# Sketch matrices loaded from GpSimd's queue, keys first on the two other load queues, eleven clock fillers in one group, and a new order of steps

## The chip, the core and the metric

The kernel runs on one core of one Trainium2 chip. The core has five engines that run side by side, each through its own list of instructions in order: TensorE (PE, matmuls; PEld is its loading of weights), VectorE (DVE), ScalarE (ACT), GpSimd (POOL) and SyncE (SP). Data comes from and goes to the chip's memory by DMA. A DMA is issued by an instruction on an engine (here on SP, ACT, and after the change also on POOL), and the issuing instruction takes time on that engine. The metric is the device time of one execution in microseconds (us).

## What is computed

Attention by polynomial sketches, followed by a feed-forward layer with a rational activation.

```python
# q, k, v: (4, 4, 1088, 32); S1, S2: (8, 32); w_in: (128, 2048); w_out: (2048, 128); float32
def phi(x):                                   # 64 features of a token
    a = np.einsum('rd,bhsd->bhsr', S1, x)
    b = np.einsum('rd,bhsd->bhsr', S2, x)
    return np.einsum('bhsi,bhsj->bhsij', a, b).reshape(*x.shape[:-1], 64)
q_p, k_p = phi(q), phi(k)
kv = np.einsum('bhsf,bhsd->bhfd', k_p, v)
z = np.sum(k_p, axis=2)
num = np.einsum('bhsf,bhfd->bhsd', q_p, kv)
den = np.einsum('bhsf,bhf->bhs', q_p, z)[..., None] + 1e-06
x = (num / den), heads side by side           # (4352, 128)
h = x @ w_in
P = a[0] + a[1]*h + a[2]*h**2 + a[3]*h**3
Q = 1.0 + abs(b[0])*abs(h) + abs(b[1])*h**2
out = (P / (Q + 1e-06)) @ w_out               # (4352, 128)
```

## The kernel before

The work comes in two interleaved streams. The attention stream goes batch by batch: keys are transposed on DVE (`kt`, L254), sketched with S1 and S2 on PE (`ks`, L261), one half is copied by ACT (`kc`, L268), the two halves are multiplied to features on DVE (`kf`, L273), and PE multiplies features with values (`kp`, L302); ACT copies the result into `kvz` (`kk`, L312). Queries go a similar way in blocks: transpose (`qt`, L325), sketch (`qs`, L338), copy (`qc`, L345 and L348), features (`qf`, L354 and L357), products with `kvz` (`qp`, L365), the division (`qd`, `qi`, `qx`), a transpose back on PE (`qb`, L391) and a copy into `xT` (`qk`, L398).

The feed-forward stream goes over 17 units of tokens and hidden columns: `h` is the matmul with w_in (L455, four parts a unit), `e` its copy to bf16 on ACT (L461), `u`, `w`, `y` build the denominator on DVE, `ln` and `ex` invert it on ACT, `pa` (ACT) or `pd` (DVE) build part of the numerator, `s`, `m`, `v`, `x` multiply on DVE, `G` is the matmul with w_out (L588), and `st` transposes and stores.

Nothing is scheduled by a planner when the kernel is built. The order of all steps is written out in the string `ORDER`, a list of `name:number` entries that a loop at the end runs through; since each engine works in order, `ORDER` fixes the order on every engine. Loads are entries as well, and are issued from SP: `lk`, `lq`, `lv` for keys, queries and values, `lx:0` and `lx:1` for the halves of w_in, `lw:0` and `lw:1` for the halves of w_out. `wo:0` to `wo:5` turn a half of w_out into one of three bf16 copies, on ACT or DVE as `W_ENG` says (1 is ACT): even numbers read the half of `lw:0`, odd numbers that of `lw:1`. `ba` makes |b| on ACT.

Ahead of the list stands a fixed opening. It loads S1 (ACT's queue) and S2 (SP's queue), then the first batch's keys in three loads, queries and values. The matrices are transposed on DVE (`sT`, L195) and masked into `S12` (L200), which the key sketches need; POOL writes the masks and some ones and zeros, and then makes `S21` (L206) and `SAB` (L212) for the query sketches. These DVE steps come ahead of every entry of `ORDER`.

`tn:i` is a group of `TURNS[i]` filler matmuls on a tile of zeros (L170) whose result nobody reads. Before the change `tn:0`, `tn:1`, `tn:4` and `tn:5` stand in the opening with 12, 2, 1 and 2 of them, 17 in all, ahead of the first key sketch on PE.

Of the kernel before, what the change touches and what calls it, by code (L numbers as in the profile page):

```python
# [16 lines left out]
PSUM = bass.MemoryType.PSUM  # L17


TURNS = (12, 2, 0, 0, 1, 2, 0, 0, 0)  # L20
ORDER = """
tn:0 lw:1 lq:0 kt0:0 lw:0 kt1:0 lx:1 tn:1 kt2:0 lx:0 tn:4 kt3:0 tn:5 lk:1 ks0:0 qt:0 qt:1 ks1:0 kc0:0 ks2:0 kf0:0
kc1:0 kf1:0 qs:0 kc2:0 kf2:0 kp0:0 qc:0 kp1:0 ba:0 qf:0 kp2:0 wo:3 qs:1 kk:0 lv:1 qt:3 qp:0 qt:2 qc:1 wo:1 lq:1 qf:1
qs:2 qd:0 qi:0 qc:2 qp:1 qx:0 qf:2 wo:0 qb:0 qp:2 qd:1 wo:4 qk:0 qi:1 h3:0 qx:1 qd:2 wo:5 wo:2 h2:0 e3:0 kt1:1 kt0:1
h0:0 e2:0 qi:2 lk:2 pa1:0 u1:0 qs:3 w1:0 h1:0 qx:2 y1:0 qc:3 e0:0 qb:2 qb:1 qt:4 e1:0 ks1:1 qt:5 qk:2 u0:0 qk:1 qs:4
ln1:0 h2:1 w0:0 qt:6 y0:0 kc1:1 ex1:0 h0:1 kf1:1 e2:1 ks0:1 s1:0 e0:1 h1:1 m1:0 kc0:1 pa0:0 kf0:1 h3:1 lq:2 kt0:2 e1:1
x1:0 e3:1 h0:2 ln0:0 u1:1 h2:2 qf:3 w1:1 qc:4 e0:2 qp:3 e2:2 kt1:2 y1:1 ex0:0 h1:2 s0:0 h3:2 ln1:1 m0:0 kp1:1 e3:2
x0:0 qd:3 e1:2 qi:3 pd0:1 ex1:1 G0:0 qx:3 lv:2 u1:2 G1:0 ln0:1 G2:0 w1:2 lk:3 G3:0 y1:2 qs:5 kk:1 ex0:1 qb:3 G4:0
ks0:2 qk:3 qf:4 G5:0 kc0:2 ln0:2 kf0:2 qp:4 s0:1 qc:5 G0:1 qd:4 ex0:2 qi:4 qx:4 G1:1 s1:1 qb:4 ks1:2 qk:4 s0:2 pa1:1
h2:3 kt1:3 m0:1 kc1:2 h3:3 qt:7 e2:3 m1:1 kf1:2 h0:3 e3:3 ln1:2 x1:1 qs:7 h1:3 x0:1 e0:3 st:0 m0:2 h2:4 e1:3 pd1:2  # L30
pa0:2 h3:4 u1:3 qf:5 e2:4 kp1:2 w1:3 qc:7 ex1:2 x0:2 h0:4 e3:4 s1:2 pa0:3 qt:9 qp:5 y1:3 e0:4 h1:4 qd:5 m1:2 ln0:3
G2:1 qi:5 x1:2 G3:1 e1:4 kt0:3 lv:3 G4:1 ex0:3 u1:4 ks0:3 G5:1 m0:3 pa1:3 G0:2 w1:4 G1:2 ln1:3 qx:5 G2:2 y1:4 qb:5
G3:2 qk:5 ex1:3 h0:5 m1:3 kk:2 v0:3 ln0:4 h2:5 s1:3 G4:2 e0:5 ex0:4 qf:7 h1:5 x0:3 e2:5 qs:6 s0:4 qc:6 e1:5 h3:5 pd0:4
pa1:4 m0:4 h1:6 v1:3 x0:4 e3:5 G5:2 e1:6 u1:5 qp:7 ln1:4 qt:8 st:2 h3:6 w1:5 ex1:4 x1:3 G0:3 e3:6 h0:6 y1:5 pa0:5 lq:3
G2:3 s1:4 h2:6 e0:6 m0:5 qd:7 ln0:5 G3:3 qi:7 m1:4 G5:3 e2:6 qf:6 qs:8 ex0:5 x1:4 G0:4 G1:4 u1:6 qc:8 ln1:5 qp:6 v0:5
qx:7 w1:6 qb:7 qd:6 pa0:6 G2:4 qi:6 G3:4 qx:6 y1:6 qb:6 qk:7 G4:4 qk:6 ex1:5 h3:7 m0:6 pa1:5 G5:4 s1:5 h1:7 e3:7 qt:10
h2:7 st:4 e1:7 m1:5 ln0:6 h0:7 x0:5 e2:7 x1:5 e0:7 h3:8 qf:8 ex0:6 u1:7 qs:9 v0:6 h1:8 qc:9 ln1:6 w1:7 ks1:3 s0:6 e1:8
G0:5 y1:7 kc1:3 ex1:6 qp:8 h2:8 pd1:6 kc0:3 e3:8 s1:6 ln0:7 h0:8 kf0:3 e2:8 m1:6 G2:5 ex0:7 x0:6 G3:5 G4:5 kf1:3 qd:8
e0:8 qs:10 G5:5 ln1:7 qi:8 u1:8 kp1:3 qx:8 pa0:7 w1:8 qf:9 qb:8 G0:6 qk:8 y1:8 qc:10 ex1:7 h3:9 s0:7 h2:9 e3:9 s1:7
ln0:8 h0:9 m0:7 e2:9 x1:6 G2:6 e0:9 h1:10 x0:7 ex0:8 pd1:7 h1:9 m1:7 pa0:8 s0:8 G3:6 e1:9 u1:9 G0:7 qt:11 ln1:8 qp:9  # L40
qt:12 u0:9 m0:8 h3:10 e1:10 w1:9 qd:9 ex1:8 qf:10 h2:10 x0:8 e3:10 x1:7 G4:6 kk:3 e2:10 h0:10 y1:9 pa0:9 w0:9 qp:10
qi:9 y0:9 e0:10 G1:7 qx:9 qd:10 ln0:9 qi:10 s1:8 qb:9 G5:6 u1:10 G2:7 qk:9 ex0:9 G3:7 qx:10 m1:8 qb:10 G4:7 qk:10
pd1:8 ln1:9 qs:11 s0:9 h1:11 qc:11 w1:10 ex1:9 h0:11 m0:9 e1:11 x1:8 G5:7 e0:11 h3:11 y1:10 pa1:9 G0:8 s1:9 e3:11
h2:11 ln0:10 x0:9 h0:12 m1:9 e2:11 pd0:10 ex0:10 h1:12 u1:11 x1:9 G1:8 ln1:10 G2:8 w1:11 G3:8 e0:12 s0:10 G0:9 e1:12
y1:11 G4:8 ex1:10 G5:8 G1:9 m0:10 ln0:11 G2:9 qf:11 h2:12 s1:10 ex0:11 x0:10 h3:12 pa1:10 m1:10 qs:12 s0:11 G3:9 qc:12
e2:12 G4:9 pd0:11 ln1:11 G5:9 m0:11 qp:11 x1:10 e3:12 G0:10 x0:11 qd:11 ex1:11 G1:10 qi:11 u1:12 G2:10 pa1:11 qx:11
G3:10 w1:12 qb:11 G4:10 qk:11 s1:11 pa0:12 h1:13 y1:12 h3:13 e1:13 m1:11 ln0:12 h2:13 st:6 x1:11 ex0:12 G5:10 qf:12
G0:11 st:10 e3:13 qp:12 s0:12 e2:13 st:8 h0:13 ln1:12 m0:12 u1:13 h2:14 e0:13 x0:12 ex1:12 u0:13 h3:14 w1:13 e2:14
w0:13 y1:13 e3:14 h1:14 qd:12 pa1:12 y0:13 h0:14 s1:12 e1:14 qi:12 m1:12 G1:11 e0:14 G2:11 qx:12 ln1:13 u1:14 G3:11
x1:12 qb:12 G4:11 ex1:13 w1:14 G5:11 G0:12 qk:12 pd0:13 ln0:13 h0:15 y1:14 ex0:13 h2:15 pd1:13 s1:13 e0:15 G1:12 s0:13  # L50
ln0:14 G2:12 h3:15 m1:13 e2:15 m0:13 ex0:14 h1:15 x1:13 x0:13 e3:15 G3:12 e1:15 G4:12 s0:14 ln1:14 G0:13 u1:15 G5:12
m0:14 h2:16 pa0:14 w1:15 h3:16 ex1:14 st:12 y1:15 G1:13 e2:16 e3:16 h1:16 x0:14 ln0:15 u2:16 u3:16 h0:16 w2:16 s1:14
ex0:15 w3:16 G2:13 y2:16 pd0:15 e1:16 G0:15 y3:16 e0:16 G3:13 s0:15 pa1:14 u0:16 G1:15 m0:15 G4:13 ln1:15 w0:16 G5:13
m1:14 G0:14 ex1:15 y0:16 G1:14 G2:14 v1:14 ln0:16 G3:14 pd1:15 s1:15 ex0:16 x0:15 x1:14 G2:15 ln2:16 m1:15 G5:14
ex2:16 s0:16 G0:16 pa0:16 x1:15 G3:15 st:14 ln3:16 m0:16 G4:15 ex3:16 s2:16 G1:16 x0:16 pa2:16 G5:15 m2:16 pa3:16
G2:16 s3:16 G3:16 x2:16 G4:16 st:15 G5:16 m3:16 G6:16 G7:16 x3:16 G8:16 st:16
""".split()
W_ENG = (1, 1, 0, 0, 0, 1)
P_ON_ACT = (1, 1, 0, 1, 1, 0, 1, 1, 0, 1, 1, 1, 1, 0, 1, 0, 1, 0, 1, 1, 0, 1, 0, 1, 1, 1, 0, 0, 1, 1, 0, 0, 1, 1)
SPLIT_A = (0, 9, 13, 16)  # L60
QUARTER = (16,)
LX = 4
TAIL = 2
WIDE_S = (3, 5)
WIDE_M = (5,)
# [4 lines left out]
def kernel(  # L70
# [13 lines left out]
    nc = tc.nc  # L84
# [53 lines left out]
    s_raw = []  # L138
    for i, s_in in enumerate((S1, S2)):
        t = consts.tile([128, D], FP, name=f"s_raw{i}")  # L140
        (nc.scalar, nc.sync)[i].dma_start(out=t, in_=bass.AP(tensor=s_in.tensor, offset=s_in.offset,
                                                             ap=[[0, 16], [D, R], [1, D]]))
        s_raw.append(t)
    nc.scalar.dma_start(out=k0.rearrange("p (m x) -> p m x", m=NM)[:, :, 0:4 * D],
                      in_=bass.AP(tensor=k.tensor, offset=k.offset, ap=[[S * D // 32, 128], [W, NM], [1, 4 * D]]))
    nc.sync.dma_start(out=k0[:, 0:km].rearrange("p (m x) -> p m x", m=NM - 1)[:, :, 4 * D:],
                        in_=k0_src[:, 0:km].rearrange("p (m x) -> p m x", m=NM - 1)[:, :, 4 * D:])
# [19 lines left out]
    def turn(i, cols=512):  # L167
        idle_ps = bank()
        for _ in range(TURNS[i]):
            nc.tensor.matmul(idle_ps[:, :cols], lhsT=idle[:, 0:128], rhs=idle[:, :cols], start=True, stop=True)  # L170
# [22 lines left out]
    for i in range(2):  # L193
        t = consts.tile([128, D], FP, name=f"sT{i}")
# [14 lines left out]
    for i in range(2):  # L209
        t = consts.tile([128, 2, R, R], FP, name=f"SAB{i}")  # L210
# [15 lines left out]
    def bank():  # L226
        return att.tile([128, 512], FP, name="att_ps")
# [211 lines left out]
    t1 = n_tok % TC  # L439
    last = TC // TAIL  # L440
    for t0, tl in [(0, t1)] * (t1 > 0) + [(t, TC) for t in range(t1, n_tok - TC, TC)] + [(t, last) for t in range(n_tok - TC, n_tok, last)]:
# [226 lines left out]
    for step in ORDER:  # L668
        name, i = step.split(":")
        i = int(i)  # L670
# [47 lines left out]
```

## Time and profile before

| | |
|---|---|
| time, median of 3 runs | 272.9 us (272.5 to 273.84) |
| the profiled execution's own time | 272.58 us |
| its span | 270.8 us |
| PE, DVE, ACT, POOL busy | 258.0, 256.8, 249.1, 2.9 us |
| granted TensorE clock | 1.0 |

The span is the time from the first to the last instruction in the profile; the execution's own time lies 1.8 us above it. Busy time is the time in which an engine works on an instruction, without its waits. The timeline lists instructions in order of time, with neighbours of one kind merged into one row ("x4"), and with the idle time ahead of a row and what ended it in brackets. The chain is followed back from the last instruction, at each step to what released it.

### The profile page before, as it was taken

How to read it: one execution, taken by the hardware profiler on the slowest of the kernel's cores; microseconds unless marked ns; L12 is line 12 of the kernel's file. 1: busy time of each engine (PE TensorE's matmuls, PEld its weight loads, DVE VectorE, ACT ScalarE, POOL GpSimd, SP SyncE). 2: the span in 40 equal slices, each digit the busy share in tenths (PEclk: the TensorE clock that was granted, in tenths of full speed). 3: DMA queues.
4: the chain of work that ended last, by engine and by line, in shares of the span. 5: the costliest groups of instructions: out<-in, count | busy, mean ns of one | idle time of the engine just before them, and what ended most of it. 6: DMA issues, size and time to landing. Idle time of an engine off the chain costs nothing.

```text
span 270.8 us, 3744 instructions
## 1 busy us (share of the span) xinstructions
PE 258.0 (95%) x1401; PEld 146.6 (54%) x1401; DVE 256.8 (95%) x278; ACT 249.1 (92%) x224; POOL 2.9 (1%) x24
## 2 busy tenths in 40 slices
PE   8999999999999899999999999999999999999673
PEld 3887546854744354535464554434545357665362
DVE  3859999999999999999999999999999999999993
ACT  1379999989999999999999999999999999999990
POOL 4000000000000000000000000000000000000000
PEclk9999999999999999999999999999999999999999
DMA  6994424532180062331303000300216100020022
GB/s 164 286 321 138 118 76 125 160 84 67 47 151 21 12 143 75 81 77 26 97 8 121 5 1 6 120 7 0 64 47 93 23 0 2 0 39 0 1 41 40
DMA packets 30530, 19.55 MB, mean 72 GB/s; under 512 B 20400, under 2 KB 26672, under 8 KB 30512
## 3 DMA queue, kind: packets, MB, share of 16 engines
q1 hardware_dynamic: 28864, 18.92, 27.5%
q10 hardware_dynamic: 1648, 0.40, 0.7%
q8 instruction: 11, 0.18, 0.3%
q14 instruction: 7, 0.06, 0.1%
HBM read 16.16 MB, written 3.15 MB: 71 GB/s over the span
## 4 chain that ended last, share of the span: by engine, by line
ACT 38%; DVE 27%; PE 25%; issue 8%; DVEq 0%; ACTq 0%
ACT hh L461 11%; ACT ln L546 10%; PE h_ps L455 9%; ACT r L550 9%; ACT p L541 7%; PE att_ps L588 7%; DVE g L558 5%; DVE g L569 5%; DVE s L554 4%; DVE w L495 4%; DVE w L490 3%; PE att_ps L365 2%; PE att_ps L170 2%; PE att_ps L302 2%; DVE u L484 2%
## 5 line engine op out<-in xcount | busy, mean ns | idle before, releaser
L455 PE MATMUL h_ps<-xT,w_in_sb 128*128 128x512 f32 (+1 forms) x320 | 125.7, 536 | 2.3 <-ACT hh L461 1.9
L455 PEld LDWEIGHTS h_ps<-xT,w_in_sb 128*128 128x128 f32 x320 | 58.4, 190 | 53.2 <-issue 36.4
L461 ACT CAST hh<-h_ps 128x1024 bf16<-128x1024 f32 x68 | 67.9, 1023 | 3.1 <-PE h_ps L455 2.8
L588 PEld LDWEIGHTS <-w_out 128*128 128x128 bf16 x460 | 44.7, 98 | 46.7 <-issue 15.7
L546 ACT ACTIVATE ln<-w 128x2048 f32<-128x2048 bf16 (+1 forms) x35 | 65.8, 1880 | 0.5
L550 ACT ACTIVATE r<-ln 128x2048 bf16<-128x2048 f32 (+1 forms) x35 | 65.8, 1880 | 0.3
L541 ACT ACTIVATE p<-hh,a_sb 128x2048 bf16<-128x2048 bf16 (+1 forms) x23 | 46.7, 2036 | 0.0
L554 DVE TENSOR_TENSOR s<-hh,r 128x2048 bf16<-128x2048 bf16 (+2 forms) x33 | 40.9, 1247 | 0.3 <-ACT r L550 0.3
L495 DVE TENSOR_TENSOR w<-w,u 128x4096 bf16<-128x4096 bf16 (+2 forms) x22 | 39.3, 1792 | 0.0
L588 PE MATMUL att_ps<-g,w_out 128*128 128x512 bf16 (+1 forms) x160 | 35.0, 347 | 4.0 <-DVE g L569 3.9
L558 DVE TENSOR_TENSOR g<-hh,s 128x2048 bf16<-128x2048 bf16 (+1 forms) x30 | 35.0, 1171 | 0.1
L569 DVE TENSOR_TENSOR g<-g,p 128x2048 bf16<-128x2048 bf16 (+1 forms) x30 | 34.9, 1179 | 0.1
L588 PE MATMUL att_ps<-r,w_out 128*128 128x512 bf16 (+1 forms) x160 | 34.5, 347 | 0.1
L588 PE MATMUL att_ps<-s,w_out 128*128 128x512 bf16 (+1 forms) x140 | 29.7, 342 | 0.4 <-DVE s L554 0.4
L490 DVE TENSOR_SCALAR w<-u,b_abs 128x4096 bf16<-128x4096 bf16 (+2 forms) x22 | 24.0, 1096 | 0.1
L484 DVE TENSOR_SCALAR u<-hh 128x4096 uint16<-128x4096 uint16 (+2 forms) x22 | 21.3, 973 | 0.4 <-ACT hh L461 0.2
L365 PEld LDWEIGHTS att_ps<-kvz,q_pT 128*128 128x128 f32 x144 | 17.7, 192 | 3.8 <-issue 1.6
L365 PE MATMUL att_ps<-kvz,q_pT 128*128 128x66 f32 x144 | 17.8, 273 | 0.4 <-ACT sk_sb L415 0.4
L302 PEld LDWEIGHTS att_ps<-v_sb,k_p 128*64 128x64 f32 (+1 forms) x288 | 8.8, 138 | 2.3 <-issue 1.5
L536 DVE TENSOR_SCALAR p<-hh,a_sb 128x2048 bf16<-128x2048 bf16 x12 | 9.7, 805 | 0.0
L273 DVE TENSOR_TENSOR k_p<-att_ps,b_sk 128x1280 f32<-128x1280 f32 (+2 forms) x8 | 9.4, 1178 | 0.0
L302 PE MATMUL att_ps<-v_sb,k_p 128*64 128x64 f32 (+1 forms) x288 | 9.3, 223 | 0.0
(60 smaller groups left out, 134.1 us busy)
## 6 DMA issues: line engine op xcount, KB each, us to landing
a_all<-sk_d SPq DMA_DIRECT2D x6, 384.0 KB
b_all<-sk_d SPq DMA_DIRECT2D x12, 192.0 KB
v_sb<-in_v_dram SPq DMA_DIRECT2D x12, 144.0 KB
k_sb<-in_k_dram SPq DMA_DIRECT2D x3, 544.0 KB
q_sb<-in_q_dram SPq DMA_DIRECT2D x3, 544.0 KB
a_all<-sk_d SPq DMA_DIRECT2D x4, 320.0 KB
b_all<-sk_d SPq DMA_DIRECT2D x8, 160.0 KB
w_out_sb_f<-in_moe_w_out_dram SPq DMA_DIRECT2D x2, 512.0 KB
```

What stands on the lines that cost most here:

```text
L365: nc.tensor.matmul(self.nd[:, o:o + 2 * KW], lhsT=self.q_p[:, c, x:x + 128], rhs=kvz[self.b % 2][:, c, :], start=True, stop=True)
L455: nc.tensor.matmul(t[:, x * tl:(x + 1) * tl], lhsT=w_in_sb[:, f * 128:(f + 1) * 128], rhs=xT[:, x_at(t0):x_at(t0) + tl], start=True, stop= ...
L461: nc.scalar.copy(out=live[i]["hh"][:, part * PW:(part + 1) * PW], in_=live[i]["h", part])
L490: nc.vector.tensor_scalar(out=t[:, c], in0=live[i]["u"][:, c], scalar1=ab1, scalar2=ab0, op0=AX.mult, op1=AX.add)
L495: nc.vector.tensor_mul(out=t[:, c], in0=t[:, c], in1=live[i]["u"][:, c])
L541: nc.scalar.activation(out=part_of(i, "p", h), in_=hh, func=ACT.Identity, scale=a3, bias=a2)
L546: nc.scalar.activation(out=t, in_=live[i]["w"][:, span(h)], func=ACT.Ln, bias=1.0 + 1e-6)
L550: nc.scalar.activation(out=part_of(i, "r", h), in_=live[i]["ln"], func=ACT.Exp, scale=-1.0)
L554: nc.vector.tensor_mul(out=part_of(i, "s", h), in0=hh, in1=part_of(i, "r", h))
L558: nc.vector.tensor_mul(out=part_of(i, "g", h), in0=hh, in1=part_of(i, "p" if horner(i, first(h)) else "s", h))
L569: nc.vector.tensor_mul(out=g, in0=g, in1=part_of(i, "s" if horner(i, first(h)) else "p", h))
L588: nc.tensor.matmul(outs[t0][:, :tl], lhsT=w_sb[y][:, f0 + x, :], rhs=part_of(i, key, h)[:, c:c + tl], start=done[0] == 0, stop=done[0] == ...
```

## The change

- S1 and S2 are both loaded from POOL's queue, ahead of everything else that the kernel puts there. The first two key loads thereby stand first on ACT's and SP's queues.
- `TURNS` has 11 fillers in `tn:0` and none elsewhere; the entries `tn:1` and `tn:5` are gone, and `tn:4` is empty.
- `ORDER` is written anew. Each step keeps its engine. A constant `SWS = 1` is added that nothing shown reads.

```diff
-TURNS = (12, 2, 0, 0, 1, 2, 0, 0, 0)
+TURNS = (11, 0, 0, 0, 0, 0, 0, 0, 0)
 ORDER = """
-tn:0 lw:1 lq:0 kt0:0 lw:0 kt1:0 lx:1 tn:1 kt2:0 lx:0 tn:4 kt3:0 tn:5 lk:1 ks0:0 qt:0 qt:1 ks1:0 kc0:0 ks2:0 kf0:0
-kc1:0 kf1:0 qs:0 kc2:0 kf2:0 kp0:0 qc:0 kp1:0 ba:0 qf:0 kp2:0 wo:3 qs:1 kk:0 lv:1 qt:3 qp:0 qt:2 qc:1 wo:1 lq:1 qf:1
-qs:2 qd:0 qi:0 qc:2 qp:1 qx:0 qf:2 wo:0 qb:0 qp:2 qd:1 wo:4 qk:0 qi:1 h3:0 qx:1 qd:2 wo:5 wo:2 h2:0 e3:0 kt1:1 kt0:1
-h0:0 e2:0 qi:2 lk:2 pa1:0 u1:0 qs:3 w1:0 h1:0 qx:2 y1:0 qc:3 e0:0 qb:2 qb:1 qt:4 e1:0 ks1:1 qt:5 qk:2 u0:0 qk:1 qs:4
+tn:0 lw:1 lq:0 kt1:0 lx:1 kt0:0 lw:0 kt2:0 lx:0 tn:4 kt3:0 lk:1 ks1:0 qt:1 ks0:0 qt:0 ks2:0 kc0:0 kc1:0 kf0:0 kf1:0
+qs:0 kc2:0 kf2:0 kp0:0 qc:0 kp1:0 qf:0 kp2:0 wo:5 qs:1 lv:1 kk:0 qt:3 qp:0 qt:2 qc:1 wo:1 lq:1 qf:1 qs:2 qd:0 qi:0
+qc:2 qp:1 qx:0 qf:2 ba:0 qb:0 qp:2 qk:0 wo:4 wo:0 wo:3 h3:0 qd:1 qd:2 wo:2 qi:1 qx:1 h2:0 qi:2 e3:0 qx:2 kt1:1 qs:3
+kt0:1 e2:0 qb:2 h0:0 qk:2 lk:2 u1:0 pa1:0 w1:0 h1:0 y1:0 qc:3 e0:0 qt:6 qb:1 qt:4 ks0:1 e1:0 qs:4 qk:1 u0:0 kc0:1
 ...
+SWS = 1
 ...
-        (nc.scalar, nc.sync)[i].dma_start(out=t, in_=bass.AP(tensor=s_in.tensor, offset=s_in.offset,
+        nc.gpsimd.dma_start(out=t, in_=bass.AP(tensor=s_in.tensor, offset=s_in.offset,
                                                              ap=[[0, 16], [D, R], [1, D]]))
```

The rest of `ORDER` holds the same entries as before, many of them a few places earlier or later.

## The prediction, made before the changed kernel was run

> **What bounds the kernel now.** I read the page first, then the busy time by stretch, the timeline of the first 26 us, and the chain of work that ended last.
>
> The page: three engines are nearly full, and GpSimd (POOL) is almost unused.
>
> ```profile
> span 270.8 us, 3744 instructions
> PE 258.0 (95%) x1401; PEld 146.6 (54%) x1401; DVE 256.8 (95%) x278; ACT 249.1 (92%) x224; POOL 2.9 (1%) x24
> ```
>
> Busy time by stretch (length, then busy us and instructions of PE, PEld, DVE, ACT, POOL, then granted clock, DMA share, GB/s): after 36 us DVE and ACT have no idle time worth naming. What can be won lies ahead of 36 us, or in the last nine.
>
> ```profile
> 0.00:17.15 17.15, 15.96 (x158) 11.44 (x158) 11.23 (x28) 6.80 (x16) 2.92 (x24) 1.00 0.88 261
> 17.15:36.00 18.85, 18.58 (x81) 12.33 (x81) 16.27 (x21) 17.18 (x19) 0.00 (x0) 1.00 0.57 151
> 120.00:150.00 30.00, 30.00 (x174) 15.26 (x173) 30.00 (x29) 29.85 (x27) 0.00 (x0) 1.00 0.23 63
> 262.00:270.80 8.80, 3.87 (x32) 3.02 (x31) 4.24 (x8) 1.59 (x2) 0.00 (x0) 1.00 0.26 38
> ```
>
> The timeline (start, duration, engine, line, what; in brackets the idle time before it and what ended it): each load's issue, the fillers (L170), the sketch matrices on DVE (L195, L200), the key transposes (L254), the query transposes (L325) and the key features (L273).
>
> ```profile
> 0.73 0.69 SPq L141 DMA_DIRECT2D s_raw<-in_S_dram  x1
> 0.74 0.64 ACTq L141 DMA_DIRECT2D s_raw<-in_S_dram  x1
> 1.19 5.45 PE L170 MATMUL att_ps<-idle 128*128 128x512 bf16 x17 [1.19 <-DVE idle L165]
> 1.41 0.60 ACTq L144 DMA_DIRECT2D k_sb<-in_k_dram  x1
> 2.90 0.49 DVE L195 STREAM_TRANSPOSE sT<-s_raw 128x32 f32<-128x32 f32 x2 [1.77 <-DMA s_raw<-in_S_dram]
> 3.31 0.30 DVE L200 TENSOR_TENSOR S<-sT,mask 128x32 f32<-128x32 f32 x2
> 4.53 1.61 PEld L170 LDWEIGHTS <-idle 128*128 128x128 bf16 x8 [0.23 <-issue]
> 4.76 1.66 DVE L254 STREAM_TRANSPOSE kT<-k_sb 128x256 f32<-128x256 f32 x4 [1.14 <-DMA k_sb<-in_k_dram]
> 6.66 0.77 DVE L325 STREAM_TRANSPOSE qT<-q_sb 128x256 f32<-128x256 f32 x2 [0.24 <-DMA q_sb<-in_q_dram]
> 7.36 1.25 DVE L273 TENSOR_TENSOR k_p<-att_ps,b_sk 128x512 f32<-128x512 f32 x2
> 8.95 1.49 DVE L273 TENSOR_TENSOR k_p<-h_ps,b_sk 128x1280 f32<-128x1280 f32 x1 [0.34 <-ACT b_sk L268]
> ```
>
> The chain (start, length, what): from the fillers on it stays on PE without a gap until 20.9 us, and then goes to ACT.
>
> ```profile
> 1.19 5.45 PE att_ps L170 x17
> 6.63 0.84 PE att_ps L261 x8
> ...
> 17.24 3.65 PE h_ps L455 x16
> 20.91 1.02 ACT hh L461
> ```
>
> So the kernel is an opening in which PE waits for nothing but its own fillers, and then some 225 us of full engines. The first key sketch starts at 6.47, while its transposed keys were there from about 5.2. A start that is earlier by x shifts all three engines by x, if nothing later is late.
>
> **Part 1: the keys go first on SP and ACT.** Two issues leave (0.69 and 0.64 us), so the first key loads are issued at 0.73 instead of 1.41 (ACT) and 1.48 (SP): 0.67 to 0.75 earlier. All that follows on these queues was spaced by issue and by the transfer stream ahead of it (the DMA share is 0.88 in the opening), so it moves too: keys landed at 4.76 and now at about 4.1, queries at 6.66 and now at 6.0, and the first w_out half, which let L625 start at 11.25, at 10.6. Later SP issues that wait for a key load to land (1.5 us in the waits of SP, before two parts of v) move with it. I take 0.65 for all.
>
> **Part 2: both sketch matrices on POOL.** No DMA of POOL is in the trace, so its cost is bounded. The two DMAs now stand one behind the other, at the head of POOL. Low end: each holds its queue as on SP and ACT (0.66), and lands as the second one did, read at 3.18, so 2.45 after its issue began: 0.73 + 0.66 + 2.45 = 3.85. High end: after two such issues a landing as slow as the queries' (issued 2.34, read 6.66, 4.3 us): 0.73 + 1.3 + 4.3 = 6.4. I take 4.4: the same bytes from the same tensor are the nearest row, but now their packets run beside the keys' instead of ahead of them. [...] No run so far shows such a DMA.
>
> On POOL, everything else stands behind these two issues, some 1.3 us: the masks (0.73 to 1.5, then to about 2.9, still ahead of the matrices that they multiply), the ones and zeros of v_sb, kvz and kT, the identity (needed at 15.9). SAB took until 1.1 us after S12 was done; it would be ready near 5.9, and the first query sketch comes at about 7.4. All hidden at these prices.
>
> **Part 3: the transposes.** DVE takes L195 and L200 in program order ahead of the keys. In the trace, from the start of the second L195 to the end of L200 was 0.43 us. So the key transposes start at T = max(4.1, 4.4 + 0.42) = 4.8, 0.04 later than before: the keys' 0.65 is lost on DVE, the sketch matrices being now what is late.
>
> **Part 4: fillers 17 to 11.** By the PEld rows the first eight start 0.427 apart, and from 4.53 on 0.216 apart. Eleven end at 4.53 + 3 x 0.216 = 5.2. The new first sketch step, ks1, needs the first transpose (T + 0.45 = 5.25). PE's own part of the gain is 6.47 - 5.25 = 1.2 us.
>
> **Part 5: what is late next.** DVE: four key transposes 1.66, two query transposes 0.77 (queries there at 6.0), key features 1.25 and 1.49: the last features end at T + 5.17, where the trace has 10.44 for T = 4.76; the saving is the waits of 0.24 (queries) and 0.34 (b_sk), since sketches now run ahead. After them come 40 of the 72 products, 2.32 x 40/72 = 1.29. The products end at T + 6.5 = 11.3; they ended at 11.95. PE alone would get there sooner (ks2 from T + 1.66, 1.12; query sketches 1.13; 32 products 1.03; sum T + 4.94), so DVE decides. Gain **0.65 us**.
>
> **Part 6: moved steps.** On ACT wo:5 (1.04) now stands ahead of kk:0, and its half of w_out lands at 10.6: kk would start at 11.65, end at 12.2, and release qp:0; PE gets to qp:0 at 11.3 + 1.13 = 12.4. Hidden, by 0.2. It leaves 17.35, where ACT had idle time, so it brings nothing. wo:3 (0.75, DVE) leaves 11.25 for the stretch after qf:2, where DVE stood idle for 2.2 us before the second batch's key transposes; those wait for their load (landed 20.39) with qi:2 and qx:2 (0.6) now ahead of them: idle time filled. qk:0 goes ahead of wo:0 (1.16) on ACT: x reaches PE earlier, but h3:0 starts when qp:2 is done, so nothing. ba:0 goes behind qc:2; b_abs is read at 22.7. On SP lx:1 goes ahead of lw:0: the w_in half is earlier, the w_out half some 1.6 us later (first read at 15.7; the load that reuses its semaphore found it landed at 13.8). After 30 us the order differs by swaps of neighbours on PE, ACT and DVE. With engines full they can remove almost nothing, and can cost where one waits; I put zero, with 0.7 us on both sides.
>
> **Sum.** h3:0, ACT's hh and all behind them come 0.65 earlier. The profiled execution took 272.58 (270.8 of span and 1.8 around it), 0.3 below the median 272.9. 272.58 - 0.65 = 271.9, at the level of the median 272.25: 272.3.
>
> **Rivals.**
>
> (a) The sketch matrices land late; slower. Place: DVE's first wait. Each us after 4.4 adds a us to T, and the gain is 5.45 - T, so the turn is a landing at 5.0; a landing at the high end, 6.4, gives T = 6.8 and costs 1.35: 274.2. At 7 it costs 1.95: 274.9. For it: two issues in a row on a queue whose price no row shows, packets beside the full key stream, small loads behind it. Against it: 16 KB landed in 2.2 us on the other queues.
>
> (b) The new order costs in the full stretch: one wait the size of L254's 2.2 us for the second batch's keys, but at a place where no engine has slack, from which all three run late: 272.3 + 2.2 = 274.5. For it: 147 of 272 DVE steps stand at another place in their order. Against: most moves are by one to five places.
>
> (c) The fillers carry more than this execution shows; faster. The rate doubled 3.3 us after the first filler. Had it done so a us later, 17 fillers would have ended 0.5 later and 11 at most 0.7 later, which T mostly hides; never, at 8.4 against 5.9. Gain 0.65 + 0.5 to 2.0: 271.7 to 270.2. [...]
>
> (d) The change does nothing: the matrices land at 5.0, the fillers' gain is eaten on DVE: 272.9.
>
> **Numbers.** 0.5%, about what a measurement of this kernel can tell from no change, is 1.4 us. Forecast 0.44 and (d) 0.10; (a) 0.20, (b) 0.13, (c) 0.13. Faster by over 0.5%: three quarters of (c), and a quarter of the forecast, where the low landing (T = 4.3, gain 1.15) meets the order's 0.7: 0.21. Slower: three quarters of (a), and most of (b): 0.26. Within: 0.53. Range 271.0 to 274.6: it leaves out the far ends of (a), (b) and (c).
>
> **What would show it.** Right: first L144 issue near 0.74; L195 of the second matrix at about 4.4 and L254 at 4.8; 11 fillers ending near 5.2; last key features ending near 10.0; products at 11.3; first L455 near 16.5; hh at 20.3; full engines after. Wrong: an L195 after 5.0, a PE gap after the fillers with slow sketches, kvz (L312) held by wo:5, or new waits on DVE or ACT after 36 us.

## The result, and the profile after

| | before | after |
|---|---|---|
| time, median (range) | 273.27 us (272.5 to 273.84, 4 runs) | 277.97 us (277.31 to 278.85, 4 runs) |
| the profiled execution | 272.58 us, span 270.8 | 278.45 us, span 276.7 |
| ratio, after over before | | 1.0168, 95% interval 1.0146 to 1.019 |

The kernel became 1.7% slower. The forecast was 272.3 us, and its range ended at 274.6.

The page of the kernel after: span and engines, the granted clock in 40 slices, and POOL's queue. The engines do as much as before (PE 259.2 us, DVE 256.2, ACT 249.2). What differs is the clock: 0.5 and 0.7 in the second and third slice, that is from 7 to 21 us, and full afterwards. The queue `q0` is the new one of POOL: 64 packets and 0.03 MB.

```profile
span 276.7 us, 3730 instructions
PE 259.2 (94%) x1380; PEld 149.5 (54%) x1395; DVE 256.2 (93%) x278; ACT 249.2 (90%) x224; POOL 4.1 (1%) x26
PEclk9579999999999999999999999999999999999999
q0 software_dynamic: 64, 0.03, 0.0%
```

The timeline of the opening after (start, duration, engine, line, what; idle time before it and what ended it). All lines are one higher than before.

```profile
0.74 0.50 ACTq L145 DMA_DIRECT2D k_sb<-in_k_dram  x1
1.19 3.88 PE L171 MATMUL att_ps<-idle 128*128 128x512 bf16 x11 [1.19 <-DVE idle L166]
1.25 1.20 POOL L142 DMA_DIRECT2D s_raw<-in_S_dram  x2 [0.81 <-POOLq L703]
...
6.48 0.21 DVE L196 STREAM_TRANSPOSE sT<-s_raw 128x32 f32<-128x32 f32 x1 [5.34 <-DMA s_raw<-in_S_dram]
...
7.75 0.21 DVE L196 STREAM_TRANSPOSE sT<-s_raw 128x32 f32<-128x32 f32 x1 [1.05 <-DMA s_raw<-in_S_dram]
...
8.10 1.48 DVE L255 STREAM_TRANSPOSE kT<-k_sb 128x256 f32<-128x256 f32 x4
...
8.59 1.97 PE L262 MATMUL att_ps<-S,kT 128*128 128x64 f32 x8 [3.52 <-DVE kT L255]
```

The keys are issued first, at 0.74, as meant. But DVE waits 5.34 us for the first sketch matrix and 1.05 for the second, so the key transposes start at 8.10 instead of 4.76. PE has done its eleven fillers at 5.07 and then stands idle for 3.5 us. Its first eight sketch matmuls take 1.97 us; the same eight took 1.00 before (0.84 of it behind the fillers, as the chain shows).

Busy time by stretch after (start:end, length, then PE, PEld, DVE, ACT, POOL busy, granted clock, DMA share, GB/s). The mean clock of 0.83 in the stretch to 8.50 puts its fall at 7.34, and the 0.70 in the stretch from 16.50 puts its return at 17.58:

```profile
5.10:8.50 3.40, 0.00 (x0) 0.00 (x0) 0.97 (x6) 0.00 (x0) 0.25 (x2) 0.83 0.84 179
8.50:12.50 4.00, 3.91 (x18) 3.91 (x18) 3.02 (x8) 0.33 (x2) 0.82 (x3) 0.50 1.04 335
12.50:16.50 4.00, 4.00 (x44) 3.06 (x45) 2.60 (x3) 1.82 (x3) 0.00 (x0) 0.50 1.02 361
16.50:18.30 1.80, 1.80 (x44) 1.73 (x42) 0.00 (x0) 0.04 (x1) 0.00 (x0) 0.70 0.10 33
18.30:25.00 6.70, 6.70 (x50) 5.70 (x51) 4.93 (x13) 4.36 (x12) 0.00 (x0) 1.00 0.61 166
```

So in the profiled execution TensorE ran at half its clock for 10.24 us, right through the attention's first sketches and products, which everything else waits for. Of the four executions, the two that took 278.5 and 278.9 us have a mean clock of 0.98, and the two that took 277.3 and 277.5 have 0.99. The chain after shows both causes, the load and the slow PE:

```profile
1.93 5.80 DMA s_raw<-in_S_dram
...
8.59 1.97 PE att_ps L262 x8
10.56 2.13 PE h_ps L262 x10
12.69 2.01 PE h_ps L339 x8
14.70 3.57 PE att_ps L303 x72
...
23.56 3.51 PE h_ps L456 x16
```

The products end at 18.27, before at 11.95: 6.3 us later. The first w_in matmuls of the chain start at 23.56, before at 17.24: 6.3 later. Behind that the two kernels run level; the last output transposes end at 272.9 instead of 267.0, which is 5.9. The whole loss is made in the first 18 us.

### The profile page after: what moved, and what is told of

Read it like the earlier page. It is cut to its first block, busy times and chain, and to the rows that moved or that the text cites. A ratio compares the mean times of both kernels' runs of the same rounds, so it can differ in the third digit from the quotient of the medians.

```text
span 276.7 us, 3730 instructions
## 1 busy us (share of the span) xinstructions
PE 259.2 (94%) x1380; PEld 149.5 (54%) x1395; DVE 256.2 (93%) x278; ACT 249.2 (90%) x224; POOL 4.1 (1%) x26
## 4 chain that ended last, share of the span: by engine, by line
PE 44%; ACT 26%; DVE 18%; issue 7%; DMA 3%; SPq 1%; POOL 0%; DVEq 0%; ACTq 0%; POOLq 0%
PE h_ps L456 18%; PE att_ps L589 14%; ACT ln L547 8%; ACT r L551 7%; ACT hh L462 7%; PE att_ps L366 4%; DVE g L559 4%; ACT p L542 4%; DVE s L555 3%; DVE w L496 3%; PE att_ps L262 2%; PE att_ps L303 2%; DMA s_raw<-in_S_dram 2%; DVE g L570 2%; PE h_ps L339 1%
## 5 line engine op out<-in xcount | busy, mean ns | idle before, releaser
L589 PE MATMUL att_ps<-g,w_out 128*128 128x512 bf16 (+1 forms) x154 | 34.1, 346 | 5.3 <-DVE g L570 4.8
L262 PE MATMUL att_ps<-S,kT 128*128 128x64 f32 x62 | 8.8, 292 | 3.5 <-DVE kT L255 3.5
L303 PEld LDWEIGHTS att_ps<-v_sb,k_p 128*64 128x64 f32 (+1 forms) x288 | 10.1, 155 | 2.3 <-DVE u L485 0.8
L262 PEld LDWEIGHTS att_ps<-S,kT 128*128 128x128 f32 x62 | 8.4, 209 | 4.9 <-DVE kT L255 4.0
L303 PE MATMUL att_ps<-v_sb,k_p 128*64 128x64 f32 (+1 forms) x288 | 10.6, 240 | 0.0
```

The lines of the kernel that those rows point to most:

```text
L303: nc.tensor.matmul(out.rearrange("p (n d) -> p n d", d=D), lhsT=self.k_p[part][:sl, t - self.PARTS[part][0], 2 * c + a].rearrange("p i j - ...
L589: nc.tensor.matmul(outs[t0][:, :tl], lhsT=w_sb[y][:, f0 + x, :], rhs=part_of(i, key, h)[:, c:c + tl], start=done[0] == 0, stop=done[0] == ...
```

## The experiments

The theory after the result had two parts: the matrices' small packets arrive late on POOL's queue because they share the DMA engines with the stream of the other loads; and the hole this leaves on PE lets the clock fall, which costs as much again. Rivals: POOL's path is slow by itself; the new order or the eleven fillers cost the time.

**The change with the matrices on their old queues**

```diff
-        nc.gpsimd.dma_start(out=t, ...      # S1, S2
+        (nc.scalar, nc.sync)[i].dma_start(out=t, ...
```

> The changed kernel with the two sketch matrices loaded as before (S1 on ACT, S2 on SP, ahead of the keys); its eleven fillers and its order stay. Theory 1 (the loss is the late landing of the matrices from POOL's queue, and the idle PE that follows): the key transposes start near 4.8 us again, the first sketch near 5.3, the products end near 11.3 instead of 18.3; 0.2 to 1 us faster than before, 272.3 to 273.1. Theory 2 (the new order or the fewer fillers cost): still 2 us or more slower than before, 275 or more.

Measured: 272.17 us (5 runs) against 273.25 of the kernel before; ratio 0.9965 (0.995 to 0.9979). The clock stays at 1.0. Putting back this one line takes away the whole loss, and the rest of the change (fewer fillers and the new order; the keys are issued as late as before) is worth 1.1 us. It beats both kernels, though the steps of its opening came later than expected: transposes at 5.29, first sketch at 5.79, end of the products at 12.53. Its timeline shows what comes next once the matrices are on time:

```profile
5.29 1.62 DVE L255 STREAM_TRANSPOSE kT<-k_sb 128x256 f32<-128x256 f32 x4 [1.66 <-DMA k_sb<-in_k_dram]
...
10.21 2.32 PE L303 MATMUL att_ps<-v_sb,k_p 128*64 128x64 f32 x72 [0.74 <-DMA v_sb<-in_v_dram]
```

The transposes wait for the keys and the products for the values: here loads decide, not DVE.

**The POOL loads alone, in the kernel before**

```diff
-        (nc.scalar, nc.sync)[i].dma_start(out=t, ...
+        nc.gpsimd.dma_start(out=t, ...
```

> The kernel before with one edit: both sketch matrices loaded from POOL's queue; 17 fillers and the old order stay. Theory 1: the matrices are read at 6.5 and 7.7 and the key transposes start near 8.1, 3.3 us late; PE is idle for 2 us only, from 6.5 to 8.6, so the clock may stay full: 275.5 to 277 if it does, up to 279 if it falls. Theory 2: within 1 us of before.

Measured: 276.01 us (4 runs), ratio 1.0105 (1.0068 to 1.0142). The matrices are read at 6.98 and 8.17. The stretch between the last filler and the first sketch:

```profile
7.04:9.11 2.07, 0.01 (x2) 0.04 (x1) 1.09 (x6) 0.00 (x0) 0.44 (x3) 1.00 0.62 154
```

With 17 fillers PE is idle for 2.07 us only, and through the opening of the profiled execution the clock stays at 1.00. The matrices are even 0.4 to 0.5 us later than after, and the price is 2.8 us instead of 4.7. The POOL loads are slow enough by themselves to make the kernel slower, without the new order.

**The change with 27 fillers**

```diff
-TURNS = (11, 0, ...
+TURNS = (27, 0, ...
```

> The changed kernel with 27 fillers instead of 11, so that PE is busy until about 8.5 us, when the first sketch can start. Theory 1a (more than half of the loss is the clock that fell while PE was idle from 5.1 to 8.6): granted clock 1.0, sketches to products 6.5 us long instead of 10.2, 3 to 4 us faster than the changed kernel: 274 to 275.3. Theory 1b (the lateness alone is the loss, the clock only shows it): within 1 us of the changed kernel, 277 to 279.

Measured: 274.55 us (4 runs), ratio 1.0056 (1.0034 to 1.0078). The matrices are as late (6.71, 7.87), but the clock stays full, and the chain has the same steps at half their length:

```profile
1.19 8.90 PE att_ps L171 x27
10.10 0.84 PE att_ps L262 x8
10.94 1.12 PE h_ps L262 x10
12.05 1.06 PE h_ps L339 x8
13.12 2.25 PE att_ps L303 x72
```

These four steps take 5.27 us; after they took 9.68. This divides the loss. From the first experiment (272.17) to this one (274.55) is 2.4 us for the late matrices; from this one to the kernel after (277.97) is 3.4 us for the clock. In the chains of the profiled executions the w_in matmuls start at 17.82, 20.66 and 23.56, which makes steps of 2.84 and 2.90 (the profiled one with 27 fillers took 275.45, 0.9 above its median). The kernel with the POOL loads alone gives much the same: 2.8 us for the lateness, which leaves 3.0 of the 5.8 that putting the line back won (if the new order gains the same in both). The 27 fillers ran until 10.09 (they start 0.43 us apart until about 7.1, and 0.22 from there) and held the first sketch to 9.94, past the about 8.7 at which its keys were there. So up to 1.2 us of the lateness share is this kernel's own, and the clock's share is some 3 us or more.

**Both matrices on SP**

```diff
-        nc.gpsimd.dma_start(out=t, ...
+        nc.sync.dma_start(out=t, ...
```

> The changed kernel with both sketch matrices on SP's queue, one behind the other ahead of SP's key load; ACT's key load still goes first. Theory 1: the matrices are read at about 2.9 and 3.8, ACT's key load now has the transfers nearly to itself and lands near 4.2, key transposes start near 4.3: 0.8 to 1.3 us faster than before, 272.0 to 272.5. Theory 2: 275 or more, as in the run with the old queues. If SP's later loads, some 0.7 us later than in the changed kernel, are what is late next: 272.8 to 273.5.

Measured: 273.14 us (272.29 to 275.8, 10 runs), ratio 1.0012 (0.998 to 1.0044). The expectation was missed. I had thought that SP would bring both in time; the second one came late there too, beside the keys that ACT had by then started:

```profile
0.73 1.32 SPq L142 DMA_DIRECT2D s_raw<-in_S_dram  x2
...
3.77 0.21 DVE L196 STREAM_TRANSPOSE sT<-s_raw 128x32 f32<-128x32 f32 x1 [2.64 <-DMA s_raw<-in_S_dram]
...
5.47 0.21 DVE L196 STREAM_TRANSPOSE sT<-s_raw 128x32 f32<-128x32 f32 x1 [1.49 <-DMA s_raw<-in_S_dram]
```

So the lateness is not POOL's alone: a second small load is late on another queue too. And the clock fell again, though PE waits for 0.35 us only ahead of its first sketch: the profiled execution (273.73 us) has a mean clock of 0.994, and the query sketches take 1.76 us (before 1.13) and the products 3.09 (before 2.32):

```profile
8.79 1.76 PE L339 MATMUL h_ps<-qT,SAB 64*128 64x256 f32 x8
...
10.82 3.09 PE L303 MATMUL att_ps<-v_sb,k_p 128*64 128x64 f32 x72 [0.27 <-DMA v_sb<-in_v_dram]
```

Three of the ten executions took 275.2 to 275.8, two of them with a mean clock of 0.988. That they lost more of the clock in the same way is likely, but they left no trace that would show it.

**The keys held until the matrices have landed**

```diff
+    for c, s in ((0, 0), (4 * D, 1), (km + 4 * D, 1)):     # ahead of the key loads
+        nc.gpsimd.tensor_copy(out=k0[:, c:c + 1], in_=s_raw[s][:, 0:1])
```

One column of each key part is first written by POOL from a matrix, so that the key loads wait for it.

> The changed kernel, but the loads of ACT and SP that follow (keys, queries, values) wait until the matrices have landed: three one-column copies on POOL into the key tile, overwritten by the key loads, stand between. Only the time at which POOL's copies can read the matrices is of interest. Traffic theory (the matrices waited for the key stream on the shared transfer engines): read at 3.4 to 3.9 and 4.0 to 4.6, that is some 1.8 to 2.1 us after the end of each issue. Path theory (POOL's way of issuing takes long by itself): about 6.4 and 7.7 as in the changed kernel, 4.5 to 5.3 us after the end of each issue. The whole kernel will be slower than the changed one, since all loads start late.

Measured, one run: the same two POOL loads, issued at the same time, are read at 3.32 and 3.88.

```profile
1.25 1.20 POOL L142 DMA_DIRECT2D s_raw<-in_S_dram  x2 [0.80 <-POOLq L705]
...
3.32 0.21 DVE L198 STREAM_TRANSPOSE sT<-s_raw 128x32 f32<-128x32 f32 x1 [2.19 <-DMA s_raw<-in_S_dram]
...
3.88 0.21 DVE L198 STREAM_TRANSPOSE sT<-s_raw 128x32 f32<-128x32 f32 x1 [0.35 <-DMA s_raw<-in_S_dram]
```

Without a stream beside them they are read 3.2 and 3.9 us sooner, a little before the times that the traffic theory gave. The time as a whole is 276.03: now the keys are late, and PE works at half rate until 9.08 us at least (the first eight sketch matmuls take 1.97 us from 7.11, as long as in the kernel after).

**Only SP's loads held**

```diff
+    nc.gpsimd.tensor_copy(out=k0[:, 4 * D:4 * D + 1], in_=s_raw[1][:, 0:1])   # ahead of SP's key load
```

> The changed kernel, but only SP's loads (the second part of the keys, queries, values) wait until the second matrix has landed; ACT's key loads run beside the matrices. Only the times at which the matrices are read are of interest. Traffic theory: between the two runs so far (3.32 and 3.88 with all loads held, 6.48 and 7.75 with none): 3.6 to 5 and 4.2 to 5.5. Path theory: 6.4 and 7.7, as in the changed kernel.

Measured, one run of 276.88 us: with half the stream the matrices are read at 4.14 and 4.95.

```profile
4.14 0.21 DVE L197 STREAM_TRANSPOSE sT<-s_raw 128x32 f32<-128x32 f32 x1 [3.00 <-DMA s_raw<-in_S_dram]
...
4.95 0.21 DVE L197 STREAM_TRANSPOSE sT<-s_raw 128x32 f32<-128x32 f32 x1 [0.60 <-DMA s_raw<-in_S_dram]
```

None beside them, half, all: 3.88, 4.95, 7.75 for the second one. The lateness goes with the traffic. Beside ACT's key loads, POOL's two loads took 2.9 and 3.0 us from issue to reading here, and SP's two in the run with both on SP 3.0 and 4.0 (SP's own keys came behind them): there POOL's are not the later ones.

**Probes: the same load in the middle of the kernel**

```diff
 ...              # two spare tiles for each of probe and probed
+            if self.b:      # in keep, where x goes to xT, for the batches after the first
+                for n, e in enumerate((nc.gpsimd, nc.sync)):
+                    nc.gpsimd.tensor_copy(out=probe[n][:, 0:1], in_=xT[...])
+                    e.dma_start(out=probe[n], in_=...S1...)
+                    nc.gpsimd.tensor_copy(out=probed[n], in_=probe[n][:, 0:1])
```

> The kernel before, with added loads of S1 into spare tiles at nine later places (one by POOL, one by SP each), each followed by a one-column copy on POOL, which is idle otherwise: it shows when the load is readable. Traffic theory: from end of issue to readable about 1.8 to 2.2 us for both queues where the transfer engines are idle, more for both where they are busy. Path theory: 4.5 us or more for POOL's and 1.8 for SP's at every place. Time of the kernel within 0.5% of before.

Measured from the start of the issue to the copy that reads it: POOL's load took 1.92 to 2.05 us in seven places (DMA share 0.03 in the four of them where it was measured), and 4.14 and 3.68 in the two where the share was 0.60 and 0.39. SP's took 2.14 to 2.21 in all nine, but the five of them where the share was measured lay in no such traffic (0.10 to 0.21). One POOL load in traffic and one without, in the timeline, and then the same two stretches:

```profile
58.86 0.68 POOL L405 DMA_DIRECT2D probe<-in_S_dram  x1 [0.31 <-POOL probe L404]
63.00 1.10 POOL L407 COPY probed<-probe 128x1 f32<-128x1 f32 x1 [3.46 <-DMA probe<-in_S_dram]
...
85.41 0.52 POOL L405 DMA_DIRECT2D probe<-in_S_dram  x1 [0.30 <-POOL probe L404]
87.34 1.76 POOL L407 COPY probed<-probe 128x1 f32<-128x1 f32 x1 [1.41 <-DMA probe<-in_S_dram]
```

```profile
58.86:63.00 4.14, 4.14 (x11) 1.63 (x9) 4.14 (x5) 3.25 (x5) 0.68 (x1) 1.00 0.60 187
85.41:87.34 1.93, 1.93 (x6) 0.94 (x5) 1.93 (x3) 1.89 (x4) 0.52 (x1) 1.00 0.03 9
```

On quiet DMA engines POOL's load was no slower than SP's (1.92 to 2.05 us at a share of 0.03, SP's 2.14 to 2.21 at 0.10 to 0.21), so the rival falls as far as a path that is slow by itself goes. Whether POOL's loads are later than SP's in the same traffic, the probes don't tell. The kernel as a whole took 276.98 us in its one run, where I had expected it within 0.5% of the kernel before. Why the probes cost that much stays open; POOL's copies of one column took 0.18 to 8.7 us.

**Eleven fillers alone, and the new order alone**

```diff
-TURNS = (12, 2, 0, 0, 1, 2, ...      # in the kernel before
+TURNS = (11, 0, 0, 0, 0, 0, ...
```

> The kernel before with 11 fillers in one group instead of 17 and nothing else. If the fillers were what held the first sketch: the first sketch at 5.2 to 5.8 instead of 6.5, and 0.4 to 1.1 us faster than before. If the run with the old queues owed its 1.1 us to the new order: no difference from before.

```diff
-        nc.gpsimd.dma_start(out=t, ...      # in the kernel after
+        (nc.scalar, nc.sync)[i].dma_start(out=t, ...
-TURNS = (11, 0, ...
+TURNS = (17, 0, ...
```

> The changed kernel with the old queues for the matrices and 17 fillers in one group: the new order alone against before. If the fillers were what held the first sketch: within 0.4 us of before. If the order was the gain: 0.6 us or more faster. If the order costs and the fillers gave more than the sum shows: slower than before.

Measured: the fillers alone 272.95 us, ratio 0.9987 (0.9978 to 0.9995, 11 runs): 0.3 us, less than expected. The chain of its opening no longer goes through the fillers (5.45 us of it before) but through the load of the values, until 9.78, and the products started at 10.03, later than before (9.63). The order alone 272.34 us, ratio 0.9964 (0.9951 to 0.9978, 6 runs): 0.9 us. Neither costs anything, so rival (b) of the prediction falls too. The order's 0.9 us is where the first experiment's 1.1 comes from; it isn't made in the opening, since DVE's idle time until 36 us is 9.1 us in both of these kernels. Over the last nine microseconds, by stretch, the fillers alone (first) and the order alone:

```profile
262.00:271.00 9.00, 3.87 (x32) 3.01 (x31) 4.70 (x8) 2.07 (x2) 0.00 (x0) 0.97 0.30 44
```

```profile
262.00:271.00 9.00, 3.89 (x32) 3.01 (x31) 4.41 (x8) 2.42 (x3) 0.00 (x0) 1.00 0.40 59
```

From 262 us to the end of each span, DVE idles for 4.5 us in the first and 4.0 in the second, so about half may be won there. Where the rest is won stays open.

**Two attempts at a better place for the loads**

```diff
-    for i, s_in in enumerate((S1, S2)):
...
-        nc.gpsimd.dma_start(out=t, ...
     nc.scalar.dma_start(out=k0...         # first two key loads
     nc.sync.dma_start(out=k0...
+    for i, s_in in enumerate((S1, S2)):
...
+        (nc.scalar, nc.sync)[i].dma_start(out=t, ...
```

> The changed kernel with the matrices on the old queues (S1 on ACT, S2 on SP), but behind the first key load of each queue instead of ahead of it. Traffic theory: small loads behind 256 and 240 KB of keys land late on these queues too, at 4.5 to 6; key transposes start at 5.2 to 6.4; 272.5 to 275, slower than the run with the matrices ahead (272.17). Path theory (only POOL is slow): read by 3.9, key transposes at 4.3 to 5; faster than that run, 271.2 to 272.

```diff
-        nc.gpsimd.dma_start(out=t, ...
+        (nc.scalar, nc.sync)[i].dma_start(out=t, ...
-    nc.scalar.dma_start(out=a_sb, ...)    # and b_sb
+    nc.gpsimd.dma_start(out=a_sb, ...)    # and b_sb, behind SAB
```

> A version meant to beat both: the changed kernel with the matrices on the old queues ahead of the keys, and instead the two tiny loads of a and b, needed only after 10 us, on POOL behind the making of SAB. ACT issues two loads less, and two of the eight semaphores that SP and ACT's loads share come free, so the last two parts of v need not wait for the keys to land. If values are what is late next in the run with the matrices ahead (its products start at 10.2, released by v): products 0.3 to 0.8 us earlier, 271.3 to 271.9. If not: 272.0 to 272.4, as that run. If a or b lands too late behind the load stream (after 11): 272.5 or more.

Measured: behind the keys 272.87 us (271.98 to 275.57, 10 runs), ratio 0.9998 (0.9968 to 1.0027); the matrices are read at 4.83 and about 5.03, as the traffic theory had it, and two of ten executions took 275.5 at a mean clock of 0.988.

```profile
1.24 0.67 SPq L146 DMA_DIRECT2D s_raw<-in_S_dram  x1
1.27 0.63 ACTq L146 DMA_DIRECT2D s_raw<-in_S_dram  x1
...
4.83 0.41 DVE L196 STREAM_TRANSPOSE sT<-s_raw 128x32 f32<-128x32 f32 x2 [3.70 <-DMA s_raw<-in_S_dram]
```

These two issues begin at the same time as POOL's first one in the kernel after (1.25), and the same first key loads went ahead of them, at 0.73. Yet they took 3.6 and 3.8 us to the reading, and POOL's 5.2 (and 5.8 for its second). Here the matrices stand ahead of the queries, the values and the third key load in the same queues; from POOL's queue they ran beside them. Whether that makes the difference, or POOL's queue gets less of a full stream, no run separates.

The other one 272.59 us, ratio 0.9977 (0.9968 to 0.9986, 10 runs); its products started at 10.10, only 0.1 us sooner than in the first experiment, and still waited for the values. Neither beats the first experiment's 0.9965. Of the places tried, the matrices do best where they were: one at the head of ACT's queue and one at the head of SP's, ahead of the keys.

## Why the prediction was wrong

**Part 2 failed, and sank the forecast.** The landing of the second matrix was put at 4.4 between ends of 3.85 and 6.4; it was read at 7.75. The value was taken from the nearest row, the same bytes on SP at the head of the queue, with the remark that packets would now run beside the keys' and not ahead of them. For that remark the forecast added 0.55 us to the low end; the stream cost 3.9 (3.88 with the keys held, 7.75 without). That the low end agrees with the 3.88 is luck: the second issue began at 1.93 and not at 1.39, and its load was read 1.95 us later and not 2.45. The high end was too low, mainly on two terms: the issues begin at 1.25 on POOL, not at 0.73, as POOL first sits idle for 0.81 us; and from the end of the second issue (2.45) to the reading it is 5.3 us, where the row of the queries gave 4.3 from an issue's start. The runs show what the stream does to the second reading: 3.88 without it, 4.95 with half of it, 7.75 in it. The forecast gave the loads a queue of their own and treated it nearly as a path of their own.

**Rival (a) had the mechanism and not the size.** Its line, T = landing + 0.42 and a cost of T − 5.45, gives 8.17 − 5.45 = 2.7 for the landing measured in the kernel after (7.75). The POOL loads alone cost 2.8 us, and their second matrix was read at 8.17, for which the line gives 3.1. So the line holds to 0.3 us where the clock stays full. The rest of the loss, some 3 us of clock, was not in the prediction: a "PE gap after the fillers with slow sketches" stands among its signs, but no price was put on it.

**Part 4 cut the cover of Part 2.** The end of the eleven fillers was forecast at 5.2 and came at 5.07, with some luck: it depends on when the rate of the fillers doubles (at 3.93 here, by the clock events, and at 4.47 before), and the same eleven ended at 5.77 to 6.07 in six other runs. The step that failed is the view of them as PE time alone: ahead of a late load, seventeen fillers kept the clock up (PE idle for 2.07 us, clock 1.00), and eleven did not (3.5 us idle, clock 0.5 from 7.34 on). The forecast put the clock at nothing; it cost about 3 us (3.4 between 27 fillers and eleven).

**Part 1: 0.65 "for all" was half right.** The queries were early as forecast (the next SP load, which waits for them, at 6.03; before 6.66). The first key part was not: the SP load that waits for it was issued at 4.97, before at 4.75, though the keys were issued 0.67 earlier. The second part gained instead (4.42 against 5.56), so the two moved by 0.46 on the mean and not by 0.65 each. Single differences of this size are not safe, though: with the loads issued as before, the key transposes, which wait for the first key part, started at 5.29 in the first experiment (before 4.76), and the SP load that waits for the queries was issued at 7.41 (before 6.66). How the loads divide the stream was not tried by itself.

**Part 5 left out the values.** With the matrices on time (first experiment) DVE's chain isn't the bound: the products wait 0.74 us for the values and end at 12.53, later than the forecast 11.3 and the 11.95 of before. The keys are issued as late as before there, and T is 5.29; the forecast's T + 6.5 would give 11.8, and the wait for the values is the rest. The gain of 0.65 by way of DVE did not come about there: the w_in matmuls start at 17.82, before at 17.24.

**Part 6, zero with 0.7 on both sides,** was mis-sized: the order alone brought 0.9 us. That the time is close to the forecast where the matrices are back (272.17 against 272.3) is therefore luck: it is the order's gain and not Part 5's. Its single claims held where they could be seen: wo:5 ran at 15.23, and `kvz` at 18.26 waited for PE and not for it; the masks were done at 3.2 (forecast 2.9) and held nothing.

Rival (c) did not occur in the kernel after: there the rate of the fillers doubled 2.7 us after the first one, earlier than the 3.3 of before. Rival (d)'s picture, matrices late enough to eat the fillers' gain, is the near side of what happened.

## What to carry to other kernels

Another issuing engine moves the instruction; the packets still met the same stream here (the second matrix read at 7.75 in it, at 3.88 without it): a small load that everything waits for belongs ahead of the big stream, and its landing time is priced from a row that lay in the same traffic. Before you thin out clock fillers, ask what happens if the load behind them comes 3 us late; here the fillers were the margin (clock 1.00 with seventeen, 0.5 from 7.34 on with eleven), and losing the clock cost about as much (2.9 to 3.4 us) as the lateness itself (2.4 to 2.8 us). And when a change has several parts, put one back at a time: here one line of it cost 5.8 us and the rest won 1.1.

## What the runs showed that was not expected

- In the kernel after, by the trace's clock events, the clock first rose at 3.93 (the clock rows read 1.00 ahead of that too, but the fillers start 0.43 us apart there, and 0.22 behind it), fell at 7.34, 3.41 us later, and came back at 17.58; 10.24 is three times 3.41. Behind an opening that always starts its fillers at 1.19 or 1.20, the first rise lay elsewhere in other runs: at 4.47 in the kernel before, and, as estimates from the spacing of the fillers, at about 5.3 with the POOL loads alone and 7.1 with 27 fillers. With the keys held the first eight sketches were still at half rate at 9.08.
- The gap on PE alone does not tell whether the clock falls. It fell at 7.34 in the kernel after, where PE had worked for 1.14 of the 3.41 us since its rise, and not with the POOL loads alone, where the fillers went on for some 1.7 us after the rise and PE was then idle for 2.07. But it also fell with both matrices on SP, behind key sketches of 1.10 us from 6.32 and 1.33 us from 7.54, and not with the matrices behind the keys, where the same sketches took 1.10 us from 5.87 and 1.33 us from 7.50. In the kernel after it stayed at 0.50 through three stretches of 3.41 us in which PE worked for 2.16, 3.42 and 3.41 us, with key sketches, with key and query sketches, and mostly with the 72 products. Whether fillers count for more than small sketches do, no run tests.
- POOL's first DMA issue starts at 1.25 us, SP's and ACT's at 0.74.
- In the probes POOL's issue took 0.52 to 0.68 us, and its load was readable after 1.92 to 2.05 on quiet DMA engines (share 0.03 where measured), SP's after 2.14 to 2.21 (share 0.10 to 0.21).
